# A spectral filter beside an MLP on one core: both outputs of the small-tile transforms in one visit over six PSUM banks

## The chip, the cores and the metric

The kernel runs on one core of a Trainium2 chip. The core has a matrix engine, TensorE (PE in the profile, PEld for its weight loads), which writes only to PSUM, a memory of eight banks of 512 float32 columns by 128 partitions; VectorE (DVE), ScalarE (ACT) and GpSimd (POOL), which work on SBUF (VectorE and ScalarE on PSUM too); and SyncE (SP), which issues most of the transfers. The metric is the device time of one execution in microseconds: 148.74 us before the change, the median of three runs (148.69 to 148.85).

## What is computed

The input has 2048 tokens of 640 columns, in bfloat16. It is normalised, goes through a spectral filter and through an MLP, and the sum of all three is the output:

```python
def _A_ref(x, w_r, w_i):
    X = jnp.fft.rfft2(x.astype(jnp.float32), axes=(-2, -1))
    X = X * (w_r + 1j * w_i)
    return jnp.fft.irfft2(X, s=(S, D), axes=(-2, -1)).astype(jnp.bfloat16)

def _B_ref(x, w1, b1, w2, b2):
    h = _gelu(jnp.einsum("bsd,df->bsf", x, w1) + b1)
    return jnp.einsum("bsf,fd->bsd", h, w2) + b2

xn = _layernorm(x, axis=-1)
return x + _A_ref(xn, A_w_r, A_w_i) + _B_ref(xn, B_w1, B_b1, B_w2, B_b2)
```

The MLP goes from 640 to 1536 columns and back. All Fourier transforms are matmuls with tables of cosines and sines.

## The kernel before

The tokens are split into 16 tiles of 128 (token 16p + c is partition p of tile c). The stages, with the letters that the code and this text use:

- Each tile is normalised (VectorE; GpSimd takes the power) and transposed, tiles 0 to 7 by TensorE (`ps<-ident` in the profile), the others by transfers. The transposed tiles are `xnT`.
- The MLP's first layer runs over five blocks of tiles (4, 2, 2, 4 and 4 tiles) and 12 chunks of columns, five matmuls each (`ps<-xnT,W`); ScalarE applies the gelu and writes `gT`. The second layer takes twelve chunks a tile (`ps<-W,gT`), 512 and 128 columns each. Its result for ten tiles (`KEEP`) is computed early and added to the residual by VectorE ("kept" tiles, `kps`, line 949); for the other six it is computed at the end.
- Stage a folds the normalised tiles along their width and transforms them over the 128 partitions (`ps<-gtab`); the results are `XV`.
- Stage b, the forward width transform (`ps<-etab,XV`), works on a group of two or three tiles of `XV` in a visit of TensorE: per tile four full matmuls of 160 columns, and then, in another tile mode of the array, four remainders on 32 rows each that run side by side. Six visits, b0 to b5. VectorE and ScalarE copy the four banks to `Xb`.
- Stage c is a 16-point transform along the tokens (`ps<-Xb,mtab`): 32 matmuls of 32 x 32 x 322 columns in a visit, in the tile mode that makes 16 small arrays of the one. It has two outputs, r = 0 and 1, and each has its own visit over four banks: c00, c01 to c30, c31. They are copied to `Y`. VectorE multiplies by the filter weights `Wf` and adds (lines 838, 842: `T`, `Z`).
- Stage d is the inverse of c (`ps<-Z,ntab`), 32 matmuls of 320 columns a visit, again two visits for the two outputs v. The copies are `U` (their buffers lie in `gtab`, `T` and `U`), and transfers transpose these back into `XV` (line 863).
- Stage e is the inverse width transform (`ps<-getab`), VectorE unfolds, and the last transform over partitions (`ps<-Wf,htab`) adds into the second layer's banks or, for kept tiles, into banks of its own. VectorE adds the residual and SP writes the tile out.

The program is written as a list of operations with costs, priorities, buffers and dependencies. A planner (`Sched`) runs once when the program is built: it takes at each step the operation that can start first, the one of highest priority among near equals, gives it a buffer or PSUM banks within its `ZONE`, and so fixes the order of each engine and the waits between engines. `LAND` holds the landing times that it assumes for transfers; they enter only the order. `CHAIN` fixes the order of the visits b, c and d. Between two visits the planner puts matmuls of the MLP ("fillers"), while VectorE and ScalarE empty the chain's banks. The chain uses banks 0 to 3; first-layer fillers (`hps`) use banks 4 to 7, and the kept second layer two banks of these at a time.

All matmuls but the transposes are issued by one helper (`mms`, line 518), and the copies by another (`copy`, lines 529 for ScalarE and 530 for VectorE), so a group in the profile is told apart by its tiles: `ps` is PSUM, `W` the weights and later the output tiles.

## Time and profile before

| what | value |
| --- | --- |
| median of three runs | 148.74 us |
| span of the profiled execution | 147.0 us |
| time outside the span | 1.7 us |
| TensorE busy | 141.9 us, 97% |
| VectorE busy | 113.3 us, 77% |
| ScalarE busy | 83.8 us, 57% |
| GpSimd busy | 23.0 us, 16% |
| first, last matmul of the chain b to d | 50 us, 104 us |

The profile is one execution with the hardware profiler on. The span goes from its first to its last instruction; the reported time is 1.7 us longer. A row of the timeline is a start, a duration, and a run of like instructions merged into one; since matmuls overlap in the array, the price of a run is the start of the next row less its own. A few records are missing from a trace; where one is missing the next row has a small gap ahead of it. The busy share of an engine says little by itself: what counts is who waits for whom.

### The profile page before, as it was taken

Reading aid. Unit: us, or ns where it says so; the run is one execution under the profiler, and the core shown is the slowest. Engines: PE = TensorE matmul, PEld = TensorE weight load, DVE = VectorE, ACT = ScalarE, POOL = GpSimd, SP = SyncE. Lnnn points to the kernel's source line nnn. Section 1 sums busy time; section 2 is a strip of 40 time slices with the busy share of each in tenths; the row PEclk is TensorE's granted clock in tenths of the full one; section 3 lists DMA queues with packets and bytes.
Section 4 is the critical chain, followed back from the end, with each engine's and each line's share of the span. In section 5 each row is a group of like instructions: output and inputs, shape, how many; then the busy total and the mean of one; then the engine's idle time right before and its main releaser. Section 6 shows DMA issues by size and latency. Waiting matters only on the chain.

```text
span 147.0 us, 4149 instructions
## 1 busy us (share of the span) xinstructions
PE 141.9 (97%) x1738; PEld 89.8 (61%) x1754; DVE 113.3 (77%) x239; ACT 83.8 (57%) x143; POOL 23.0 (16%) x50
## 2 busy tenths in 40 slices
PE   7999999999999999999999999999999999999993
PEld 7899568898655655656455455334456666566573
DVE  2968999999999254979654796496206999999991
ACT  3123998899989875442878373697766324010300
POOL 4320111420000499400000000000006300000000
DMA  4899999999878899992015205606353951332233
GB/s 128 291 307 409 363 235 224 362 195 170 145 142 159 227 216 252 266 269 71 4 26 116 41 4 115 66 17 122 79 116 73 228 140 45 109 121 89 89 136 92
DMA packets 28995, 23.00 MB, mean 156 GB/s; under 512 B 17840, under 2 KB 25776, under 8 KB 28848
## 3 DMA queue, kind: packets, MB, share of 16 engines
q1 hardware_dynamic: 26640, 17.48, 48.3%
q0 software_dynamic: 2336, 5.25, 15.7%
q8 instruction: 14, 0.23, 0.6%
q14 instruction: 5, 0.04, 0.1%
HBM read 13.54 MB, written 2.62 MB: 110 GB/s over the span
## 4 chain that ended last, share of the span: by engine, by line
PE 93%; DVE 2%; DMA 2%; issue 1%
PE ps L518 92%; PE ps L690 2%; DMA X<-in_A_x_dram 2%; DVE stats L639 1%; DVE U L670 0%; DVE mv L642 0%; DVE W L958 0%
## 5 line engine op out<-in xcount | busy, mean ns | idle before, releaser
L518 PE MATMUL ps<-xnT,W 128*128 128x512 bf16 (+2 forms) x384 | 57.1, 300 | 0.0
L518 PE MATMUL ps<-W,gT 128*128 128x512 bf16 (+3 forms) x382 | 55.5, 292 | 1.4 <-issue 0.9
L518 PEld LDWEIGHTS ps<-W,gT 128*128 128x128 bf16 x396 | 29.9, 98 | 22.9 <-issue 1.9
L518 PEld LDWEIGHTS ps<-xnT,W 128*128 128x128 bf16 x384 | 31.8, 98 | 17.5 <-issue 2.0
L763 ACT ACTIVATE gT<-ps,b1col 128x512 bf16<-128x512 f32 (+1 forms) x60 | 35.0, 616 | 6.1 <-PE ps L518 5.1
L943 POOL DMA_DIRECT2D xnT<-in_A_x_dram x8 | 9.9, 2792 | 51.1 <-DMA XV<-U 51.1
L529 ACT ACTIVATE Wf<-ps 128x960 bf16<-128x960 f32 (+1 forms) x8 | 6.7, 869 | 17.6 <-PE ps L518 17.6
L639 DVE BATCH_NORM_STATS2 stats<-X 128x6 f32<-128x320 bf16 x32 | 13.7, 465 | 2.0 <-DMA X<-in_A_x_dram 2.0
L529 ACT ACTIVATE Xb<-ps 128x960 bf16<-128x960 f32 (+1 forms) x8 | 9.1, 1169 | 6.9 <-PE ps L518 6.7
L838 DVE TENSOR_TENSOR T<-Y,Wf 128x1288 bf16<-128x1288 bf16 x16 | 12.3, 823 | 0.0
L529 ACT ACTIVATE Y<-ps 128x644 bf16<-128x644 f32 x9 | 6.3, 707 | 7.5 <-PE ps L518 7.5
L949 DVE TENSOR_TENSOR X<-ps,X 128x640 f32<-128x640 f32 x8 | 6.5, 819 | 5.0 <-PE ps L518 5.0
L943 POOL DMA_DIRECT2D X<-in_A_x_dram x8 | 7.2, 2080 | 19.4 <-DMA Wf<-in_A_w_i_dram 19.4
L644 POOL TENSOR_TENSOR rstd<-mv,mhalf 128x2 f32<-128x2 f32 (+1 forms) x10 | 6.6, 663 | 20.9 <-DVE mv L642 20.9
L709 DVE TENSOR_TENSOR T<-T 128x512 bf16<-128x512 bf16 (+1 forms) x32 | 8.3, 314 | 0.1
L530 DVE CAST Xb<-ps 128x640 bf16<-128x640 f32 (+1 forms) x4 | 4.3, 1067 | 5.1 <-PE ps L518 5.1
L958 DVE TENSOR_TENSOR W<-ps,xnT 128x640 bf16<-128x640 f32 (+2 forms) x10 | 6.9, 686 | 1.1 <-PE ps L518 1.0
L530 DVE CAST Y<-ps 128x644 bf16<-128x644 f32 x7 | 5.8, 822 | 2.4 <-PE ps L518 2.4
L842 DVE TENSOR_TENSOR Z<-T 128x644 bf16<-128x644 bf16 x16 | 7.0, 486 | 0.8 <-PE ps L518 0.8
L518 PE MATMUL ps<-etab,XV 32*128 32x160 bf16 (+1 forms) x128 | 7.2, 232 | 0.0
L529 ACT ACTIVATE XV<-ps 128x256 bf16<-128x256 f32 (+4 forms) x9 | 6.8, 751 | 0.5 <-PE ps L518 0.5
L897 DVE TENSOR_TENSOR Wf<-Wf 128x960 bf16<-128x960 bf16 (+1 forms) x12 | 6.8, 593 | 0.3 <-ACT Wf L529 0.2
(59 smaller groups left out, 145.6 us busy)
## 6 DMA issues: line engine op xcount, KB each, us to landing
X<-in_A_x_dram POOLq DMA_DIRECT2D x8, 320.0 KB, 6.8
xnT<-in_A_x_dram POOLq DMA_DIRECT2D x8, 320.0 KB, 8.7
out_dram<-W SPq DMA_DIRECT2D x15, 160.0 KB, 1.8
X<-in_A_x_dram SPq DMA_DIRECT2D x6, 320.0 KB, 8.5
W<-in_B_w_dram SPq DMA_DIRECT2D x4, 480.0 KB, 10.4
W<-in_B_w_dram SPq DMA_DIRECT2D x6, 192.0 KB, 3.8
Wf<-in_A_w_r_dram SPq DMA_DIRECT2D x7, 160.5 KB, 10.3
Wf<-in_A_w_i_dram SPq DMA_DIRECT2D x7, 160.5 KB, 9.7
```

Source lines behind the costliest of these rows:

```text
L518: ins = e.matmul(o_, lhsT=lw, rhs=rh, start=st, stop=sp_, skip_group_check=True)
L529: return e.activation(dst(), src(), ACT.Copy, scale=scale)
L530: return e.tensor_copy(dst(), src())
L639: o = K.op([("dve", 0.393)], pr, lambda e, _, c=c, h=h: e.bn_stats(stats[:, c, 6 * h:6 * h + 6], view(X, c * D + H2 * h, [[1, H2]])), read ...
L644: K.op([("pool", 0.65)], 500, lambda e, _, a=a, b=b: e.tensor_tensor(out=rstd[:, a:b], in0=mv[:, a:b, 1], in1=mhalf[:, a:b], op=ALU.pow), ...
L709: ring_ops.append(K.op([("dve", dve_us(4 * w, 2))], pr, lambda e, _, op=op, x1v=x1v, xfv=xfv, o_=o_, o0=o0, o1=o1, w=w: e.tensor_tensor(ou ...
L763: g_op = K.op([("act", act_us(128 * nt, 1))], pr + PRIO["gelu"] + GP[bi], lambda e, _, c0=c0, nt=nt, fc=fc, hps=hps: e.activation(gT[:, fc ...
L838: filt_ops.append(K.op([("dve", dve_us(4 * KP, 2))], pr, lambda e, _, k=k, Y=Y, TB=TB, pair=pair: e.tensor_tensor(out=view(TT, TB.slot * 8 ...
L842: K.op([("dve", dve_us(2 * KP, 2))], pr, lambda e, _, TB=TB, Z=Z, r=r, op=op: e.tensor_tensor(out=view(Zb, Z.slot * 4 * KP + r * KP, [[2 * ...
L897: K.op([("dve", dve_us(320 * n, 2))], pr + 2, lambda e, _, k=k, op=op, yo=yo, y2=y2, n=n: e.tensor_tensor(out=view(Wf, Y2 + y2.slot * 3 * ...
L943: xo_ops[c] = K.op([("pool", 0.9)], 51 - c / 20, lambda e, _, c=c, xov=xov: e.dma_start(xov(0, D), xv[:, c, :], accum_op=ALU.add), reads=[ ...
L958: K.op([("dve", dve_us(w))], 95, lambda e, _, os_=os_, fps=fps, o0=o0, w=w, xov=xov, base=base: e.tensor_tensor(out=view(W1, OST + os_.slo ...
```

## The change

1. *c and d, one visit each per four tiles.* Both outputs are computed in one visit of 96 matmuls over six banks. Four banks hold the first output of 322 (or 320) columns and half of the second one; the other halves, 160 columns each, lie two to a bank in banks 4 and 5. The two halves of the array's rows write to those banks in turn, so the visit is cut into twelve runs of eight matmuls (`M_RUNS`, `N_RUNS`). Its third run ends with an increment of a new semaphore of TensorE, and its ninth run waits for it (`mark`).
2. *b by four tiles.* Four visits of four tiles for six of two or three. The fourth tile's columns lie in banks 4 and 5; the remainders are ordered so that row groups do not meet in a bank, with one more such wait between the first round and the fourth. The fourth tile of `Xb` lies in free places of `T` and `gtab`. Two memsets of their padding join the start, two follow stage a.
3. *Copies.* Each b, c and d visit is emptied by four operations, two for the four banks and two for banks 4 and 5.
4. *Fillers of one bank.* The chain's zone is banks 0 to 5. First-layer fillers of the last two blocks and the kept second layer have banks 6 and 7. A kept tile is computed in two halves of 320 columns, each in one bank, each added by VectorE.
5. *Order.* `CHAIN` has 12 entries for 22. `RANK` gives every operation a new priority, from a search; `LAND` has new values. The order changes everywhere.

```diff
+RANK = """
+428 732 735 708 725 420 419 730 734 329 592 297 284 335 376 299 399 300 279 374 448 364 231 406 222 503 503 503 393 503 503 503 503 503 503 503 503 503 503 503 503 503
...
+""".split()
...
     def schedule(self):
+        for o, r in zip(self.ops, RANK, strict=True):
+            o.prio = int(r)
...
-ZONE = {"hps": [(4, 8)], "bps": [(0, 4)], "cps": [(0, 4)], "dps": [(0, 4)],
-        "eps": [(0, 4)], "fin": [(4, 8), (0, 4)], "fps": [(4, 8)], "tps": [(0, 2), (2, 8)], "aps": ANY, "h0": [(2, 8)], "h1": ANY}
+ZONE = {"hps": [(4, 8)], "hpc": [(6, 8)], "bps": [(0, 6)], "cps": [(0, 6)], "dps": [(0, 6)],
+        "kps": [(6, 8)], "eps": [(0, 4)], "fin": [(4, 8), (0, 4)], "fps": [(4, 8)], "tps": [(0, 2), (2, 8)], "aps": ANY, "h0": [(2, 8)], "h1": ANY}
...
-CHAIN = 'b0 b1 c01 c00 b2 c10 c11 b4 d01 d00 b3 c20 c21 d11 d10 b5 c30 d21 c31 d20 d30 d31'.split()
+CHAIN = 'b0 c0 b1 c1 d0 b2 c2 d1 b3 c3 d2 d3'.split()
...
+M_RUNS = [(0, 0, 0, 0, KP, True), (1, 1, 0, 1, 160, True), (1, 1, 1, 1, 160, False), (0, 0, 1, 0, KP, False), (1, 0, 0, 0, KP, True), (0, 1, 0, 0, 162, False), (1, 0, 1, 0, KP, False),
+          (0, 1, 1, 0, 162, False), (0, 1, 0, 1, 160, False), (1, 1, 0, 0, 162, False), (0, 1, 1, 1, 160, False), (1, 1, 1, 0, 162, False)]
...
         def mms(lst):
             def f(e, _):
-                for o_, lw, rh, st, sp_ in lst():
+                for o_, lw, rh, st, sp_, *mark in lst():
+                    if mark == [1]:
+                        e.wait_ge(K.bank, K.banks)
                     ins = e.matmul(o_, lhsT=lw, rhs=rh, start=st, stop=sp_, skip_group_check=True)
+                    if mark == [0]:
+                        K.banks += 1
+                        ins.then_inc(K.bank, 1)
                 return ins
             return f
...
+        def mark(h, a, b, x, k):
+            return ((1,) if (h, b, k) == (0, 0, 0) else (0,) if (h, b, k) == (1, 1, 7) else ()) if x else ()
...
+        def four(slot, lhs, tab):
+
+            def at(i, g):
+                return psb(slot + g, [[1, Q4]], Q4 * i) if i < 3 else psb(slot + 4 + g // 2, [[1, Q4]], Q4 * (g % 2))
+            main = [(at(i, g), lhs(i, g, 0, 128), tab[:, Q4 * g:Q4 * g + Q4], i == 0 or (i == 3 and g % 2 == 0), False) for g in range(4) for i in range(4)]
+            return main + [(at(i, g), lhs(i, 4, 32 * g, 32), tab[32 * g:32 * g + 32, 4 * Q4:5 * Q4], False, True, *((k // 3,) if (k, g) in ((0, 3), (3, 0)) else ()))
+                           for k in range(4) for g in range(4) for i in [(k - g % 2) % 4]]
...
-            for r in range(2):
-                cps = Buf(f"cps{P}_{r}", psum, 4, ZONE["cps"])
-                zone[f"c{P}{r}"] = pe([("small", 0.335)], PRIO["pc"] - P / 2 + 0.02 * r, lambda P=P, r=r, cps=cps: [
...
+            cps = Buf(f"cps{P}", psum, 6, ZONE["cps"])
+            zone[f"c{P}"] = pe([("small", 0.64)], PRIO["pc"] - P / 2, lambda P=P, cps=cps: [
...
+                for hi, r, v, x, w, st in M_RUNS for pp in range(2) for qq in range(2) for lo in range(2)],
...
+                for x in range(2):
+                    K.op([("act", act_us(320 if x else 968)), ("dve", dve_us(320 if x else 968))], PRIO["pc"] - two[pp] / 5,
...
-                    kps = Buf(f"kps{c}", psum, 2, ZONE["fps"])
...
+                    for o0 in (0, H2):
+                        kps = Buf(f"kps{c}_{o0}", psum, 1, ZONE["kps"])
...
+                        kept_ops.append(K.op([("dve", dve_us(H2))], 30, lambda e, _, kps=kps, xov=xov, o0=o0: e.tensor_tensor(
+                            out=xov(o0, H2), in0=psb(kps.slot, [[1, H2]]), in1=xov(o0, H2), op=ALU.add), reads=[kps, xo1], writes=[xo]))
```

Three places of the new order. The first is TensorE at the start, where tiles 0 to 3 are transposed (`ps<-ident`, tiles 0 and 1 from `U`, 2 and 3 from `T`) among the first layer's matmuls. Before:

```order
L690 MATMUL ps<-ident,U 128x128 x5
L518 MATMUL ps<-xnT,W 128x128 x30
L690 MATMUL ps<-ident,T 128x128 x5
L518 MATMUL ps<-xnT,W 128x128 x6
L518 MATMUL ps<-xnT,W 128x256 x6
L518 MATMUL ps<-xnT,W 128x128 x24
L690 MATMUL ps<-ident,T 128x128 x5
L518 MATMUL ps<-xnT,W 128x128 x12
```

After:

```order
L728 MATMUL ps<-ident,U 128x128 x3
L551 MATMUL ps<-xnT,W 128x128 x30
L551 MATMUL ps<-xnT,W 128x256 x6
L728 MATMUL ps<-ident,T 128x128 x5
L551 MATMUL ps<-xnT,W 128x128 x12
L728 MATMUL ps<-ident,T 128x128 x5
L551 MATMUL ps<-xnT,W 128x128 x44
```

Tile 2's transposes (the first from `T`) moved behind the six matmuls of 256 columns, and the next twelve matmuls already use tile 2.

The second place is TensorE in the chain, around the first visits of d and the b visit behind them. Before (d01, d00, b3):

```order
L518 MATMUL ps<-xnT,W 128x512 x5
L518 MATMUL ps<-Z,ntab 32x320 x32
L518 MATMUL ps<-xnT,W 128x512 x5
L518 MATMUL ps<-Z,ntab 32x320 x32
L518 MATMUL ps<-xnT,W 128x512 x8
L518 MATMUL ps<-etab,XV 128x160 x24
L518 MATMUL ps<-xnT,W 128x512 x2
```

After (d0, b2):

```order
L551 MATMUL ps<-W,gT 128x320 x12
L551 MATMUL ps<-xnT,W 128x512 x5
L551 MATMUL ps<-Z,ntab 32x320 x8
L551 MATMUL ps<-Z,ntab 32x160 x16
L551 MATMUL ps<-Z,ntab 32x320 x16
L551 MATMUL ps<-Z,ntab 32x160 x8
L551 MATMUL ps<-Z,ntab 32x320 x8
L551 MATMUL ps<-Z,ntab 32x160 x40
L551 MATMUL ps<-W,gT 128x320 x21
L551 MATMUL ps<-etab,XV 128x160 x32
L551 MATMUL ps<-W,gT 128x320 x15
```

Two visits of 32 with a filler between them became one of 96, and b takes 32 matmuls for 24.

The third place is VectorE behind the first b visits: it copies b's banks to `Xb` (the fourth tile to `T`), adds a kept tile (`X<-ps,X`), copies c's banks to `Y`, and filters (`T<-Y,Wf`). Before:

```order
L530 CAST Xb<-ps 128x2x2x160
L530 CAST Xb<-ps 128x3x2x160
L949 TENSOR_TENSOR X<-ps,X 128x640 x2
L530 CAST Y<-ps 128x2x322
L838 TENSOR_TENSOR T<-Y,Wf 128x1288 x3
```

After:

```order
L566 CAST Xb<-ps 128x3x2x160
L566 CAST T<-ps 128x2x160
L1011 TENSOR_TENSOR X<-ps,X 128x320
L566 CAST Y<-ps 128x2x160 x2
L895 TENSOR_TENSOR T<-Y,Wf 128x1288 x3
```

One b visit with two copies on VectorE and half a kept tile stand there for two visits with one copy each and two tiles; the large copies to `Y` are ScalarE's.

More of the change, by code (lines that the diff above doesn't have):

```diff
@@ L380, in emit @@
                     o.sem, o.count = sems[e], n
+        self.bank, self.banks = nc.alloc_semaphore("s_bank"), 0
         block = es.enter_context(nc.Block())
@@ L503, in bass_parallel_sum__spectral_gfnet__dense_activation_gelu__prompt_kernel @@
         OST, REM = 0, 4 * D
+        XB3 = 16 * KP + 2 * D
         def psb(slot, dims, off=0, p0=0, n=128):
@@ L793, in bass_parallel_sum__spectral_gfnet__dense_activation_gelu__prompt_kernel, with xbv @@
+        def xbv(xb, i):
+            return (xb3, (xb.slot * 3 + i) * 2 * KP) if i < 3 else (gtab, 2 * D) if xb.slot else (TT, XB3)
+        for k, n in ((KP - 2, 3), (2 * KP - 1, 1)):
+            K.op([("pool", 0.1)], 99, lambda e, _, k=k, n=n: e.memset(view(gtab, 2 * D + k, [[1, n]]), 0.0), writes=[B_xbpad], after=a_ops)
+        for gi in range(4):
+            c0 = 4 * gi
             xb = Buf(f"xb{gi}", p_xb)
-            bps = Buf(f"bps{gi}", psum, 4, ZONE["bps"])
-            pb_ops.append(pe(five_segs(n, 0.07 * n + 0.014), PRIO["pb"] - c0 / 10, lambda c0=c0, n=n, bps=bps: five(
-                bps.slot, n, lambda i, g, p0, k: part(XV, p0, k, 2048 * g + 128 * (c0 + i), [[1, 128]]), etab),
+            bps = Buf(f"bps{gi}", psum, 6, ZONE["bps"])
+            pb_ops.append(pe(five_segs(4, 0.07 * 4 + 0.014), PRIO["pb"] - c0 / 10, lambda c0=c0, bps=bps: four(
+                bps.slot, lambda i, g, p0, k: part(XV, p0, k, 2048 * g + 128 * (c0 + i), [[1, 128]]), etab),
@@ L844, in bass_parallel_sum__spectral_gfnet__dense_activation_gelu__prompt_kernel @@
             B_us = [Buf(f"u{pair}") for pair in two]
[L845 to L854 removed]
+            dps = Buf(f"dps{P}", psum, 6, ZONE["dps"])
```

71 lines of the change are left out of this document (38 added, 33 removed), and 18 rows, old and new, of the table RANK.

## The prediction

> **What bounds the kernel now.** I read the page first: the busy shares, the slices, and the chain that ended last.
>
> ```profile
> span 147.0 us, 4149 instructions
> PE 141.9 (97%) x1738; PEld 89.8 (61%) x1754; DVE 113.3 (77%) x239; ACT 83.8 (57%) x143; POOL 23.0 (16%) x50
> ...
> PE   7999999999999999999999999999999999999993
> ...
> PE 93%; DVE 2%; DMA 2%; issue 1%
> PE ps L518 92%; PE ps L690 2%; DMA X<-in_A_x_dram 2%; DVE stats L639 1%; DVE U L670 0%; DVE mv L642 0%; DVE W L958 0%
> ```
>
> TensorE is busy in every slice from the second to the last but one, and 92% of the chain lies on line 518, which issues nearly all its matmuls. The next view is the waits of TensorE alone.
>
> ```profile
> PE ps L518 <- issue: 1.1, 7, 0.2
> ```
>
> Beside it the view has only a wait at the very start: after that TensorE waits for no engine. (The 1.1 us of "issue" stand where a record of a matmul is missing.) So the time is a start, one dense stream of matmuls, and a short tail. The sum is made against the profiled execution: span 147.0 us, 1.7 us below the 148.74 us median; I take that 1.7 us and the tail after the last matmul as unchanged. A shorter stream shortens the time one for one; a faster VectorE or ScalarE gives nothing; a new wait of TensorE adds one for one. TensorE's timeline in two stretches of the spectral chain gives the prices; the first column is the start, so a price is one start less the one before.
>
> ```profile
> 68.35 1.31 PE L518 MATMUL ps<-etab,XV 128*128 128x160 bf16 x24
> 69.59 1.80 PE L518 MATMUL ps<-W,gT 128*128 128x512 bf16 x12
> 71.23 1.24 PE L518 MATMUL ps<-xnT,W 128*128 128x512 bf16 x5
> 72.41 0.51 PE L518 MATMUL ps<-Z,ntab 32*32 32x320 bf16 x32
> 72.85 1.25 PE L518 MATMUL ps<-xnT,W 128*128 128x512 bf16 x5
> 74.06 0.52 PE L518 MATMUL ps<-Z,ntab 32*32 32x320 bf16 x32
> 74.51 1.90 PE L518 MATMUL ps<-xnT,W 128*128 128x512 bf16 x8
> 76.25 1.31 PE L518 MATMUL ps<-etab,XV 128*128 128x160 bf16 x24
> ...
> 88.26 0.98 PE L518 MATMUL ps<-etab,XV 128*128 128x160 bf16 x16
> 89.17 1.80 PE L518 MATMUL ps<-W,gT 128*128 128x512 bf16 x12
> 90.90 0.49 PE L518 MATMUL ps<-Xb,mtab 32*32 32x322 bf16 x32
> 91.33 1.90 PE L518 MATMUL ps<-xnT,W 128*128 128x512 bf16 x8
> ```
>
> A 512-column matmul costs 0.217 us (8 of them from 74.51 to 76.25), so 0.42 ns a column. Six pairs of 512 and 128 columns cost 1.64 us between full matmuls (69.59 to 71.23) and 1.73 us ahead of a small-tile visit (89.17 to 90.90): entering costs 0.09 to 0.10 us. A c visit then takes 0.43 us (90.90 to 91.33) and a d visit 0.44 to 0.45 us (72.41 to 72.85), and 0.01 us more falls on the first full matmul behind it. Of this, columns are two rounds of 322 at 0.42 ns, 0.27 us. What a visit costs beyond its columns is therefore 0.09 + 0.43 + 0.01 - 0.27 = 0.26 us for c, and 0.28 us for d.
>
> **The change, part by part.** *One c and one d visit where there were two.* The columns stay, the fixed part is paid once: 4 x 0.26 + 4 x 0.28 = 2.16 us saved. *Four width visits for six.* These rows give the price of 160 and of 320 columns.
>
> ```profile
> 140.65 0.98 PE L518 MATMUL ps<-W,gT 128*128 128x320 bf16 x6
> 141.46 0.43 PE L518 MATMUL ps<-Wf,htab 128*128 128x512 bf16 x2
> ...
> 142.68 0.99 PE L518 MATMUL ps<-W,gT 128*128 128x160 bf16 x12
> 143.51 0.23 PE L518 MATMUL ps<-Wf,htab 128*128 128x160 bf16 x1
> ```
>
> A 160-column matmul costs 0.069 us (12 in 0.83). A tile of a width visit is four of them and one more time slot for its four 32-row remainders, which run side by side: 0.346 us. The three-tile visit at 68.35 took 1.24 us and the two-tile one at 88.26 took 0.91 us, so the fixed part is 0.20 and 0.22 us, with the 0.01 us behind it 0.22 us. Two fewer visits save 0.44 us. *One-bank fillers.* Two 320-column matmuls cost 2 x 0.135 us (six in 0.81), the 512 and 128 pair 0.273 us (1.64/6): nothing, for all ten tiles. Saved in all: 2.60 us.
>
> *The wait inside a visit.* TensorE now waits for its own semaphore once in each b, c and d visit, because two row groups share a bank there; the matmul that waits, and all that is queued behind it on TensorE, stands until an earlier matmul of the same visit has ended. No wait of this kind is in the trace; the nearest rows are its two halves.
>
> ```profile
> L518 PE MATMUL ps<-Xb,mtab 32*32 32x322 bf16 x256 | 4.0, 301 | 0.0
> L518 PE MATMUL ps<-etab,XV 32*128 32x160 bf16 x64 | 2.2, 231 | 0.0
> ...
> 52.31 1.31 PE L518 MATMUL ps<-etab,XV 128*128 128x160 bf16 x24
> 53.67 1.25 DVE L530 CAST Xb<-ps 128x960 bf16<-128x960 f32 x1 [1.51 <-PE ps L518]
> ...
> 57.45 0.49 PE L518 MATMUL ps<-Xb,mtab 32*32 32x322 bf16 x32
> 58.05 0.71 ACT L529 ACTIVATE Y<-ps 128x644 bf16<-128x644 f32 x1 [0.85 <-PE ps L518]
> ...
> 5.33 0.28 DVE U L670
> 5.61 0.05 issue
> 5.65 0.39 PE ps L690 x2
> ```
>
> A reader starts 0.11 us after the last small-tile record ends (57.94 to 58.05) and 0.05 us after the last 32-row one (53.62 to 53.67); TensorE starts 0.04 us after a release (5.61 to 5.65). In a c or d visit the signal comes from the last matmul of the third run of eight, which starts some 0.12 us in (16 issues of about 3 ns and one pass of 160 columns); its record of 160 columns lasts 0.301 less 0.07, 0.23 us; less the reader's own start, of which I take 0.02 us, the ninth run can start at 0.12 + 0.23 + 0.13 = 0.48 us. Its own turn, behind two rounds of 322 and two of 162 columns (0.41 us) and some 0.03 us of issue, is at 0.44 us. That is 0.04 us for each of eight visits, 0.32 us. In a width visit the signal leaves with the first round of remainders and is needed by the fourth: 0.01 + 0.231 + 0.07 = 0.31 us against a turn at 3 x 0.07 = 0.21 us, so 0.10 us, four times, 0.40 us. Ends for both kinds together: nothing, if the signal leaves before the modelled end of a record, and 0.2 us each, 2.4 us in all, if TensorE's queue fills anew behind the wait. I take the small values: the start 0.04 us behind a release is the same engine and the same step.
>
> [...]
>
> *The start.* In the new order tile 2's transposes stand directly ahead of their first use, where six matmuls of 128 columns and six of 256 stood between.
>
> ```profile
> 9.12 0.44 PE L690 MATMUL ps<-ident,T 128*128 128x128 bf16 x5
> 9.40 2.49 PE L518 MATMUL ps<-xnT,W 128*128 128x128 bf16 x36
> 11.73 0.44 PE L690 MATMUL ps<-ident,T 128*128 128x128 bf16 x5
> ...
> 12.05 0.29 DVE L530 COPY xnT<-ps 128x256 bf16<-128x256 bf16 x1 [0.34 <-PE ps L690]
> ```
>
> Unhindered, the first use comes 12.05 + 0.29 + 0.04 - 11.73 = 0.65 us after the first transpose, of which the five transposes fill 0.28 us (9.12 to 9.40). The stall is 0.37 us; the old order lost some 0.05 us at tile 3 (six matmuls between), which goes. I put down 0.30 us, with 0 and 0.4 us as ends.
>
> *The evacuations.* Six banks are filled at once and have to be emptied before the next visit may write them; what is late next after the switches are the copies out of PSUM.
>
> ```profile
> 51.28 0.89 ACT L529 ACTIVATE Xb<-ps 128x640 bf16<-128x640 f32 x1
> 53.67 1.27 ACT L529 ACTIVATE Xb<-ps 128x960 bf16<-128x960 f32 x1 [0.53 <-PE ps L518]
> ...
> 104.86 2.52 SPq L863 DMA_TRANSPOSE XV<-T  x2
> ...
> 111.40 1.74 ACT L529 ACTIVATE W<-XV 128x384 bf16<-128x384 bf16 x2 [2.19 <-DMA XV<-U]
> ```
>
> After b0 each of two engines copies three tiles and one: 1.27 us and, by the step from 640 to 960 columns, about 0.51 us: 1.78 us. With 0.05 us to start and 0.04 us to release, c0 may start 1.87 us after b0's last record ends. TensorE's filler there is five 512s and six 320s, 5 x 0.217 + 6 x 0.135 = 1.9 us. It just fits. Behind the last d visit the transposes of four outputs, 1.3 us of issue each, and their landing take 111.40 - 104.86 = 6.5 us; with the evacuation of the larger part of an output ahead of them (768 and 192 columns, some 1.1 us by the 0.71 us for 644) and 0.1 us to start, 7.7 us. The filler between d3 and e0 is 51 matmuls of 320, five of 512 and three pairs, 6.9 + 1.1 + 0.8 = 8.8 us: also covered. If a cover is gone, the price is the difference. For the few places with less than 0.2 us to spare I put down 0.10 us in all, with 0 and 1.0 us as ends.
>
> *The rest.* Ten adds of 640 columns become twenty of 320 on VectorE, 1 to 2 us more work. VectorE sat idle 5.0 us ahead of the old ones, waiting for TensorE, which hides it:
>
> ```profile
> L949 DVE TENSOR_TENSOR X<-ps,X 128x640 f32<-128x640 f32 x8 | 6.5, 819 | 5.0 <-PE ps L518 5.0
> ```
>
> On VectorE's queue these adds stand ahead of copies out of Y's banks, and they wait for transfers of POOL's queue; counted at the prices above, b0 comes 0.8 us later in the stream than before, so these transfers have no less time. SP's weight loads and token transposes trade places far ahead of their users. Four memsets more on POOL, 16% busy, cost nothing.
>
> Sum: -2.60 + 0.32 + 0.40 + 0.30 + 0.10 = -1.48 us, 147.26 us; I say 147.3 us.
>
> **The rivals.** *The waits cost nothing* and all is covered: -2.60 + 0.30, 146.4 us. For it: the records' ends are modelled. Against: a reader has never started before such an end.
> *Each matmul has a price of its own* in the issue: eight visits of 96 for sixteen of 32 are 256 more, and the 0.16 us that a c visit of 0.43 us takes beyond its columns bounds the price at 5 ns: 1.3 us on top, 148.5 us. For it: nothing shows how much of the 0.16 us is issue. Against: width visits with 8 or 12 small matmuls have a fixed part nearly as large, 0.22 us. [...]
> *The wait drains the array*, so that each c and d visit pays its fixed part twice: the 2.16 us are lost, and the 0.32 us with them are contained in that, -0.44 + 0.40 + 0.30 + 0.10 = +0.36 us, 149.1 us, slower. It decides from about 0.23 us a visit on (0.04 + 1.48/8). For it: nothing in the trace shows a wait of TensorE on itself in mid visit. Against: after a release it starts in 0.04 us, and the tile mode does not change.
> *The two filler banks run short.* Fillers had four banks and now have two, and the gelu that empties one stands in ScalarE's queue behind the wider Y copies. There are eleven gaps in the chain; from 1.48/11 = 0.13 us a gap the gain is gone, at 0.3 us the time is 147.3 + 3.3 = 150.6 us. For it: ScalarE is in these copies for 0.7 to 1.3 us at a time. Against: TensorE never waited for a bank before, and a bank takes 1.1 us or more to fill.
>
> **How the numbers follow.** Less than 0.2%, 0.3 us, is about what a measurement of this kernel cannot tell from no change. My forecast (146.7 to 148.0 us) has 57%; hidden waits 13%; a price per matmul 7%; the drain, slower, 9%; short banks 10%, of which 4% end within 0.2% and 6% slower; something else late, a transfer above all, 4%, slower. Faster 0.77, same 0.04, slower 0.19. From 146.2 to 149.3 us only the short banks at their worst, half of the 4% and a tail below are left out, some 13%.
>
> **What would show it.** Right: TensorE's timeline has c and d visits of 0.70 to 0.78 us from start to next start, width visits of 1.6 to 1.75 us, a gap of 0.35 us near 10.5 us after tile 2's transposes, and no other wait; the span is near 145.5 us. Wrong: visits of 0.9 us or more (drain), waits of TensorE for ScalarE's gelu or copies between visits (banks), or a gap ahead of e0 that a transfer ends.

## The result, and the profile after

The change makes the kernel slower: 155.71 us median of four runs (155.24 to 156.63) against 148.73 us, a ratio of 1.047 [1.044, 1.051]. The forecast was 147.3 us, with a range that ended at 149.3 us. The profiled execution has a span of 153.9 us, 6.9 us above that of before. Its page:

```profile
span 153.9 us, 4697 instructions
PE 146.6 (95%) x2004; PEld 100.2 (65%) x2010; DVE 116.5 (76%) x257; ACT 80.2 (52%) x139; POOL 23.1 (15%) x54
...
PE   7999999983999999999999999999999999999993
...
PEclk9999999998699999999999999999999999999999
...
PE 77%; DVE 15%; DMA 4%; issue 1%; POOL 1%
```

TensorE was busy in every slice but the ends before; now it has a hole in the ninth and tenth slices (8 and 3 in the row of PE), and the granted clock (the row PEclk) is low in the tenth and eleventh (8 and 6). The chain that ended last is no longer TensorE alone: up to the hole it runs through VectorE and a transfer. The waits of TensorE name that transfer:

```profile
PE ps L551 <- DMA xnT<-U: 2.7, 1, 2.7
...
PE ps L551 <- issue: 0.3, 2, 0.2
```

It is the transpose of tile 15, from SP's queue, which the first layer of the last block of tiles needs. TensorE's timeline there:

```profile
33.51 0.71 PE L551 MATMUL ps<-xnT,W 128*128 128x256 bf16 x5
36.96 7.90 PE L551 MATMUL ps<-xnT,W 128*128 128x512 bf16 x33 [2.74 <-DMA xnT<-U]
...
49.76 1.00 PE L551 MATMUL ps<-gtab,T 128*128 128x128 bf16 x15
```

and the windows of 2 us over it (the columns: length, busy time and count of PE, PEld, DVE, ACT, POOL, then the granted clock of TensorE, the DMA share and GB/s):

```profile
34.00:36.00 2.00, 0.22 (x3) 0.00 (x0) 1.54 (x6) 1.25 (x2) 0.00 (x0) 1.00 1.23 113
36.00:38.00 2.00, 1.04 (x6) 0.62 (x7) 1.97 (x8) 0.00 (x0) 0.39 (x1) 0.92 0.71 157
38.00:40.00 2.00, 2.00 (x6) 0.70 (x5) 1.97 (x7) 1.80 (x4) 0.42 (x1) 0.50 0.93 157
40.00:42.00 2.00, 2.00 (x10) 0.95 (x9) 0.66 (x2) 1.18 (x3) 0.00 (x0) 0.72 1.30 199
```

The wait is 2.7 us, and behind it the mean granted clock is 0.50 from 38 to 40 us and 0.72 from 40 to 42 us: 2 x 0.50 + 2 x 0.28 = 1.6 us of lost work. So 4.3 of the 6.9 us are lost here, long before the part of the program that the change is about.

The visits themselves, in the same timeline (start, duration; b0 and the filler behind it, c0 from its first matmul to the filler behind it, then a filler and d0):

```profile
56.03 1.78 PE L551 MATMUL ps<-etab,XV 128*128 128x160 bf16 x32
57.74 1.25 PE L551 MATMUL ps<-xnT,W 128*128 128x512 bf16 x5
...
59.74 0.32 PE L551 MATMUL ps<-Xb,mtab 32*32 32x322 bf16 x6
...
60.84 2.33 PE L551 MATMUL ps<-xnT,W 128*128 128x512 bf16 x10
...
71.77 1.24 PE L551 MATMUL ps<-xnT,W 128*128 128x512 bf16 x5
72.95 1.20 PE L551 MATMUL ps<-Z,ntab 32*32 32x320 bf16 x96
```

The c visit takes 60.84 - 59.74 = 1.10 us from start to next start; the prediction said 0.70 to 0.78, and "wrong" from 0.9 on. The d visits take 1.13 to 1.16 us, and one c visit took 1.52 us. With 0.10 us to enter and 0.01 us behind, and less the columns (0.54 us), the eight visits cost 6.05 us beyond their columns; the sixteen of before cost 4.4 us. That is 1.6 us more, where 1.84 us less (2.16 saved, 0.32 for the wait) were expected. Of the 1.6 us some 0.4 is one gap in the visit of 1.52 us, whose cause is another (below); 1.2 us are left to the visits themselves. The b visit takes 57.74 - 56.03 = 1.71 us, inside the predicted 1.6 to 1.75.

So the 6.9 us are: 4.3 for the late transpose and the clock behind it, 1.6 for the c and d visits, 0.4 to 0.5 for the start, and some 0.5 that is spread.

### The profile page after: what moved, and what is told of

It is laid out like the page before. It is cut to its first block, busy times and chain, and to the rows that moved or that the text cites. A ratio compares the mean times of both kernels' runs of the same rounds, so it can differ in the third digit from the quotient of the medians.

```text
span 153.9 us, 4697 instructions
## 1 busy us (share of the span) xinstructions
PE 146.6 (95%) x2004; PEld 100.2 (65%) x2010; DVE 116.5 (76%) x257; ACT 80.2 (52%) x139; POOL 23.1 (15%) x54
## 4 chain that ended last, share of the span: by engine, by line
PE 77%; DVE 15%; DMA 4%; issue 1%; POOL 1%
PE ps L551 76%; DVE stats L677 6%; DMA xnT<-U 3%; DVE T L743 2%; DVE T L747 2%; DMA X<-in_A_x_dram 2%; DVE U L708 1%; DVE mv L680 1%; DVE xnT L566 1%; POOL rstd L682 1%; PE ps L728 1%; DVE XV L566 1%; DVE T L708 0%; DVE W L1020 0%
## 5 line engine op out<-in xcount | busy, mean ns | idle before, releaser
L551 PE MATMUL ps<-W,gT 128*128 128x320 bf16 (+3 forms) x390 | 56.8, 294 | 0.5 <-issue 0.3
L551 PEld LDWEIGHTS ps<-W,gT 128*128 128x128 bf16 x396 | 34.6, 98 | 18.2 <-ACT gT L801 0.2
L747 DVE TENSOR_TENSOR T<-T 128x128 bf16<-128x128 bf16 (+1 forms) x32 | 8.7, 316 | 5.0 <-PE ps L551 4.8
L1011 DVE TENSOR_TENSOR X<-ps,X 128x320 f32<-128x320 f32 x16 | 7.8, 487 | 5.6 <-PE ps L551 5.4
L565 ACT ACTIVATE Y<-ps 128x968 bf16<-128x968 f32 (+1 forms) x8 | 6.4, 839 | 3.8 <-PE ps L551 3.8
L566 DVE CAST Y<-ps 128x320 bf16<-128x320 f32 (+1 forms) x8 | 4.9, 655 | 4.6 <-PE ps L551 4.6
L566 DVE CAST Wf<-ps 128x960 bf16<-128x960 f32 (+1 forms) x5 | 5.4, 1085 | 2.7 <-PE ps L551 2.6
L566 DVE CAST Xb<-ps 128x960 bf16<-128x960 f32 x4 | 4.9, 1232 | 3.2 <-PE ps L551 3.2
L551 PE MATMUL ps<-etab,XV 128*128 128x160 bf16 (+1 forms) x128 | 7.1, 233 | 0.0
L551 PE MATMUL ps<-Wf,htab 128*128 128x512 bf16 (+3 forms) x33 | 7.0, 296 | 0.0
```

Source lines behind the costliest of these rows:

```text
L551: ins = e.matmul(o_, lhsT=lw, rhs=rh, start=st, stop=sp_, skip_group_check=True)
L565: return e.activation(dst(), src(), ACT.Copy, scale=scale)
L566: return e.tensor_copy(dst(), src())
L747: ring_ops.append(K.op([("dve", dve_us(4 * w, 2))], pr, lambda e, _, op=op, x1v=x1v, xfv=xfv, o_=o_, o0=o0, o1=o1, w=w: e.tensor_tensor(ou ...
L1011: kept_ops.append(K.op([("dve", dve_us(H2))], 30, lambda e, _, kps=kps, xov=xov, o0=o0: e.tensor_tensor(out=xov(o0, H2), in0=psb(kps.slot, ...
```

## The experiments

Two theories followed. One: TensorE cannot issue 96 small matmuls as fast as their columns would allow. Two: the new order asks for the transposes too early. The rivals: the self-wait or the shared banks make the visits slow; the stall in front is only a symptom.

**What a small matmul costs.** The first kernel leaves the old order, banks and visits as they are, has no wait inside, and only cuts each c and d matmul in two.

```diff
-(psb(cps.slot + 2 * pp + hi, [[1, KP]], 0, 64 * qq + 32 * (lo ^ pp), 32),
+(psb(cps.slot + 2 * pp + hi, [[1, 161]], 161 * y, 64 * qq + 32 * (lo ^ pp), 32),
...
-for v in range(2) for pp, qq, hi, lo in tiles],
+for v in range(2) for y in range(2) for pp, qq, hi, lo in tiles],
```

> The kernel before, with every c and d matmul cut into two of half the columns (161 or 160): 64 matmuls a visit for 32, the same columns, banks and outputs, and no wait inside. Theory A, TensorE issues small matmuls quickly (some 3.3 ns apart) only up to about 32, and then one every 8.5 ns: the last of 64 starts 32 x 8.5 ns = 0.27 us later than the 32nd, of which some 0.1 us lie beside columns, so a visit takes 0.6 us for 0.43, and 16 of them add 2.4 us or more: 151 us (150.5 to 153). Rival B, issue is not what makes the new visits slow (their shared banks or the wait are): 32 more matmuls of 3.3 ns at most, hidden beside the columns, and the time stays within 0.5 us of 148.7.

Measured: 154.96 us median (153.53 to 155.15), a ratio of 1.038 [1.032, 1.045]. This is slower than either theory said. Its timeline at a c visit:

```profile
55.28 0.76 PE L518 MATMUL ps<-Xb,mtab 32*32 32x161 bf16 x64
55.98 1.80 PE L518 MATMUL ps<-W,gT 128*128 128x512 bf16 x12
```

A visit takes 55.98 - 55.28 = 0.70 us for 0.43, so 0.27 us more for 32 more matmuls and the same columns; sixteen of them make 4.3 us. (The remaining 2 us are two gaps, which make one c visit 1.08 us and one b visit 0.34 us longer, and a wait of 0.8 us for VectorE; the gaps are explained below.) The second kernel keeps the 64 matmuls and makes the 33rd wait for the 32nd:

```diff
-for o_, lw, rh, st, sp_ in lst():
+for k, (o_, lw, rh, st, sp_) in enumerate(lst()):
+    half = len(lst()) == 64
+    if half and k == 32:
+        e.wait_ge(K.bank, K.banks)
     ins = e.matmul(o_, lhsT=lw, rhs=rh, start=st, stop=sp_, skip_group_check=True)
+    if half and k == 31:
+        K.banks += 1
+        ins.then_inc(K.bank, 1)
```

> The kernel with the halved c and d matmuls (64 a visit), with one wait more in each visit: the 33rd matmul waits for a signal of the 32nd. Theory A, TensorE's sequencer hands on some 32 pairs of weight load and matmul that were queued while the matmuls ahead ran, and feeds the rest at 8.35 ns apiece: while the 33rd waits, the queue fills behind it, so the last 32 start 3 to 4 ns apart and not 8.35 (0.10 to 0.15 us from the 33rd to the 64th, for 0.258); the wait itself costs a pass and the signal's way, so the 33rd starts some 0.45 to 0.5 us into the visit for 0.267, and a visit takes 0.75 to 0.85 us for 0.694. Rival B, it is the array or the bank, not the feed, that makes the later matmuls slow: they stay 8.35 ns apart behind the wait too, and a visit takes 0.9 us.

```profile
55.09 0.36 PE L522 MATMUL ps<-Xb,mtab 32*32 32x161 bf16 x32
55.64 0.36 PE L522 MATMUL ps<-Xb,mtab 32*32 32x161 bf16 x32 [0.20 <-PE ps L522]
55.94 1.80 PE L522 MATMUL ps<-W,gT 128*128 128x512 bf16 x12
```

The two halves have the same length, 0.36 us; a visit takes 0.85 us, and the one run 157.13 us. The third kernel is the changed one with its c and d matmuls cut to 16 columns:

```diff
-(psb(cps.slot + (4 + pp if x else 2 * pp + hi), [[1, w]], (160 * hi if x else r * KP), 64 * qq + 32 * (lo ^ pp), 32),
+(psb(cps.slot + (4 + pp if x else 2 * pp + hi), [[1, 16]], (160 * hi if x else r * KP), 64 * qq + 32 * (lo ^ pp), 32),
```

> The changed kernel, with every matmul of the c and d visits cut to its first 16 columns: the 96 matmuls, their banks and the wait inside stay, most of the columns of stages c and d are not computed. Theory A, the issue sets the length of a visit: 32 x 3.3 ns and 64 x 8.5 ns make 0.65 us, with some 0.1 us to enter and 0.1 us to end about 0.8 us, so a visit falls only from 1.1 to 0.75 to 0.95 us. Rival B, the columns or the meeting of row groups in a bank set it: a visit falls to 0.45 us or less, eight of them by 5 us in all.

```profile
70.65 0.93 PE L551 MATMUL ps<-Z,ntab 32*32 32x16 bf16 x96
71.51 1.26 PE L551 MATMUL ps<-W,gT 128*128 128x320 bf16 x8
```

A visit with a twentieth to a tenth of the columns still takes 0.86 us, as theory A said (the one run: 153.09 us). From the records of the traces, the median over all visits of a kernel, when the k-th matmul of a visit starts (us from its first):

```
kernel                        16th   17th   32nd   33rd   last   next full matmul
before, 32 a visit            0.050  0.149  0.202    -      -    0.444
halved, 64                    0.050  0.082  0.134  0.267  0.526  0.695
halved, with the wait, 64     0.050  0.081  0.135  0.556  0.692  0.854
16 columns, 96                0.050  0.065  0.122  0.205  0.755  0.864
changed kernel, 96            0.050  0.109  0.175  0.334  0.961  1.130
```

The first 16 start 3.3 ns apart in every kernel (0.050/15). Behind the 32nd there is a pause of 0.08 to 0.16 us, and from the 33rd on they start 8.3 ns apart in the halved kernel ((0.526 - 0.267)/31) and 8.7 ns with 16 columns, so columns do not set it. With the wait ahead of the 33rd, those behind it start 4.4 ns apart again ((0.692 - 0.556)/31), their 0.136 us equal to the 0.134 us of the first 32, as theory A said of this kernel. So the array can take them quickly. A reading that fits, an estimate from these numbers, is that some 32 pairs of weight load and matmul are ready ahead and a further pair comes each 8.3 ns: the pace changes behind the 32nd pair in all three kernels that have more and no wait there. No trace shows such a store itself, and what sets the pause behind the 32nd was not tried. The old visits have 32, and so never showed what more of them would cost. In the changed kernel 64 of 96 matmuls lie beyond: at the 8.3 ns of the halved kernel 64 x 8.3 = 0.53 us of the visit's 1.13, and 0.334 + 63 x 0.0083 = 0.86 us stand as a floor for the start of the last one; the pass itself takes 0.17 us more. The remaining 0.1 us are short steps at the ninth run, where the self-wait stands, and at changes of width.

**What the late transposes come from.** The planner had taken the transposes of tiles 12 to 15 to land about 3 us after their issue; they took 7.39, 5.61, 5.53 and 3.95 us. The next kernel only tells it so.

```diff
-"xnT12#0": 3.04, "xnT13#0": 2.93, "xnT14#0": 3.55, "xnT15#0": 2.94
+"xnT12#0": 7.39, "xnT13#0": 5.61, "xnT14#0": 5.53, "xnT15#0": 3.95
```

> The changed kernel, with one thing other: the planner is told that the transposed tiles 12 to 15 land 7.39, 5.61, 5.53 and 3.95 us after their transfers are issued (what the profile of the changed kernel shows) instead of 3.04, 2.93, 3.55 and 2.94. Theory A, the order took these transfers for faster than they are: the 2.74 us in which TensorE waits for a transposed tile near 34 us goes, and with it the 1.5 us or so that the lowered clock (0.74 between 38 and 44 us) cost: 155.7 - 4.3 = 151.4 us (150.6 to 152.4), and the granted clock stays at 0.97 or more in every 2 us stretch between 30 and 45 us. Rival B, the stall is only a symptom and TensorE would run into the next late thing: 155.7 us, less 1 us at most. The c and d visits stay as they are (1.1 us) by both.

Measured: 155.41 us (154.88 to 158.47), a ratio of 1.043 [1.036, 1.049]: theory A fell in this form. The order came out much the same, and the transposes went out 1.1 us later than before, so that the wait stayed. (Its profile is of the execution of 158.47 us, with a mean granted clock of 0.989; the four others had 1.00, and their waits are not on record.) SP's queue of the changed kernel, then of this one, and its wait:

```profile
19.30 4.14 SPq L544 DMA_DIRECT2D W<-in_B_w_dram  x4
26.41 4.44 SPq L717 DMA_TRANSPOSE xnT<-T  x2
30.90 3.30 SPq L717 DMA_TRANSPOSE xnT<-U  x2
```

```profile
27.55 4.67 SPq L717 DMA_TRANSPOSE xnT<-T  x2
32.27 3.30 SPq L717 DMA_TRANSPOSE xnT<-U  x2
```

```profile
PE ps L551 <- DMA xnT<-U: 2.5, 1, 2.5
```

In both, four transposes take 7.8 us and more of SP's time, though the last of them takes 1.28 us in the changed kernel. What stands ahead of them are the weights of the second layer, 1.9 MB. In the kernel before, the first two transposes behind these weights took even longer, but TensorE waited for none:

```profile
24.77 5.53 SPq L679 DMA_TRANSPOSE xnT<-T  x2
```

The next kernel issues the weights behind the transposes:

```diff
+        for o in w2_ops:
+            o.gate.append(TD[15])
         K.schedule()
```

> The changed kernel, with one thing moved: the four loads of the second layer's weights (480 KB each), which stand on SP's queue directly ahead of the transposes of tiles 12 to 15, are issued behind the transpose of tile 15; nothing needs these weights before 51 us. All else has the same order up to the chain. Theory A, the transposes are late because they are issued and move behind 1.9 MB of weights (2.0 to 2.3 us of issue each for the first three, where an undisturbed one takes 1.28): issued from 26.4 us at 1.28 us apiece tile 15's goes out at 30.3 us, 2.6 us sooner than the 32.9 us of the changed kernel, and lands near 34 us, where TensorE first needs it: the wait of 2.74 us shrinks to 0.5 us or less, the clock stays at 1.00, and the time is 155.7 - 4.2 = 151.5 us (150.8 to 152.2). Rival B, the transposes take their time whatever stands ahead of them, or the weights now come too late: the wait of 2 us or more stays or moves to the second layer, 154.5 us or more. By both the time stays above 148.7 us, since the c and d visits stay at 1.1 us.

```profile
26.27 2.62 SPq L719 DMA_TRANSPOSE xnT<-T  x2
28.94 2.60 SPq L719 DMA_TRANSPOSE xnT<-U  x2
31.59 2.17 SPq L544 DMA_DIRECT2D W<-in_B_w_dram  x4
```

```profile
33.41 6.76 PE L551 MATMUL ps<-xnT,W 128*128 128x256 bf16 x38
...
45.10 1.00 PE L551 MATMUL ps<-gtab,T 128*128 128x128 bf16 x15
...
69.05 0.71 PE L551 MATMUL ps<-Z,ntab 32*32 32x320 bf16 x45
71.81 0.92 PE L551 MATMUL ps<-Z,ntab 32*32 32x160 bf16 x51 [2.05 <-issue]
72.66 4.26 PE L551 MATMUL ps<-W,gT 128*128 128x320 bf16 x21
```

The mechanism was right: the transposes take 1.3 us each, TensorE does not wait, and the fifteen matmuls that began at 49.76 us begin at 45.10, 4.7 us sooner. The time is 155.87 us (155.52 to 156.20) all the same, ratio 1.048 [1.044, 1.051]; the number of theory A was missed by 4.4 us. The gain is lost again by 81 us, where the third c visit begins at 80.60 us for 80.79: TensorE stands 2.05 us in the middle of the first d visit, waiting for nothing that the profile shows, then the mean granted clock is 0.72 from 70 to 74 us and 0.85 from 74 to 78 us, and ahead of that TensorE waits 0.7 us near 57 us.

**What TensorE waited for in mid visit.** Such a gap, "issue" in the view of waits, is in most kernels of this study: 0.43 us in the changed one (a c visit of 1.52 us), 0.41 and 1.17 us in the halved, 0.80 us in the one with 16 columns, each from the start of one matmul or weight load to the next. By the counts, TensorE's instructions come by a queue of their own (q8, "instruction", 16 KB at a time; it has 14 such transfers before, 16 in the changed and 18 in the halved kernel, whose pages count 3492, 4014 and 4532 matmuls and weight loads, one transfer for each 256 begun). Counted from the first (a weight load, a matmul and a wait for a semaphore in TensorE's records are one each), the gaps lie as follows; "in hand" is the time from the begin of the transfer of the next 16 KB to the last instruction before the gap, "asked late" the time from the entry into the block before to the begin of that transfer:

```
kernel                  instructions done   gap    in hand   asked late
changed                 1473                0.43   1.81      5.72
halved                  1473                0.41   1.82      3.58
halved                  1729                1.17   1.13      4.95
16 columns              2241                0.80   1.79      1.41
weights late            1729                2.31   0.14      4.94
changed, next block     1729                0      4.02      1.04
before, its shortest    1473                0      5.51      2.41
```

1473, 1729 and 2241 differ by whole multiples of 256. TensorE goes on 2.2 to 2.6 us after the transfer began in all five (gap and time in hand together). The reading that fits is that it ran out of instructions: the table has them in blocks of 256, the transfer of the next block beginning while the current one runs. In the kernel before no gap lies at such a boundary in the chain (5.51 us in hand at the least); two things differ here. The visits of 96 use a block in as little as 3.6 us (80.81 to 84.40 us in the changed kernel, 3.2 us in the one with 16 columns), where before it lasted 6.5 us and more in the chain. And a transfer that begins 1.0 to 1.6 us after the block before it is entered at five other boundaries of the changed kernel (transfers between 54.33 and 85.67 us) began up to 5.7 us after. What stood in the DMA queues then, in the kernel with the late weights from the entry into the block (64.4 us) to the transfer (69.35 us), and from there to the end of the gap:

```profile
q0 software_dynamic: 576, 1.31, 112.7%
...
X<-in_A_x_dram POOLq DMA_DIRECT2D x1, 320.0 KB, 7.4
```

```profile
q0 software_dynamic: 221, 0.49, 80.0%
q8 instruction: 1, 0.02, 2.2%
```

Beside the one transfer of instructions only GpSimd's transfers of the residual, whose packets took 112.7% and then 80.0% of the 16 engines' time. Two kernels on top of the late weights spread these out: the first makes them wait for the additions of the kept tiles, the second lets no more than two be under way.

```diff
+        for i, t in enumerate(KEEP[3:]):
+            xo_ops[t].deps.append(kept_ops[2 * i + 1])
```

> The kernel with the late weights, and GpSimd's transfers of the residual spread out: from the fourth kept tile on, each waits for the addition of the kept tile three before it, so that they no longer stand in the DMA queues all at once between 56 and 71 us. TensorE's instructions have the same order. Theory A, TensorE ran out of instructions: its gaps in mid visit (2.31 us at 69.49 us with the late weights, 0.43 us at 67.89 us in the changed kernel) lie where its 1729th or 1473rd instruction ends, a whole number of 256 apart, and the transfer of the next 16 KB of instructions had begun only 0.14 and 1.81 us before, 4.9 and 5.7 us after the block before was entered, behind GpSimd's transfers; elsewhere it begins some 1 us after. With those spread out no such transfer begins more than 2.5 us after its block is entered, no gap over 0.2 us lies at such a boundary, the granted clock is 1.00 in every 4 us stretch from 50 us on, and the time falls by the 2.3 us and the 1.5 us that the lowered clock cost behind it: 155.9 - 3.8 = 152.1 us (151.0 to 152.8). Rival B, the gap has another cause (the wait of TensorE on itself, a filter step of VectorE): it stays in the visit of d0, 155 us or more.

```diff
+        seq = list(KEEP) + [t for t in range(16) if t not in KEEP]
+        for a, b in zip(seq, seq[2:]):
+            xo_ops[b].deps.append(xo_ops[a])
```

> The same with another spreading: each of GpSimd's residual transfers waits for the landing of the one two before it, so that at most two are in flight. Theory A: the same, no gap at a block's end and 152.1 us (151.0 to 153.0); a transfer that is needed by a kept tile may come late, which would show as a wait of TensorE for VectorE's addition. Rival B: 155 us or more, with the gap in mid visit.

With the first, no transfer of instructions in the chain begins more than 2.3 us after its block is entered, the visit of d0 takes 1.13 us, and the longest gap at a block's end is 0.30 us (2.30 us in hand). But a new wait took the place of the old one, for the addition of the first kept tile, whose transfer GpSimd held back (TensorE's wait, and GpSimd's queue):

```profile
PE ps L551 <- DVE X L1013: 2.9, 1, 2.9
```

```profile
54.62 2.72 POOL L1006 DMA_DIRECT2D X<-in_A_x_dram  x3 [6.03 <-DMA Wf<-in_A_w_i_dram]
```

Its executions scatter from 152.99 us, with a mean granted clock of 1.00, to 157.75 us, with 0.976, so that no ratio can be given; the mechanism of theory A held but for the 0.30 us, its number did not. The second gave 154.34 us (152.69 to 157.35); its three executions with a mean granted clock of 1.00 took 152.69 to 154.34 us, ratio 1.030 [1.025, 1.034]. In its profile, which is of the execution of 157.35 us, the gap moved from block 1729 to block 2241 and was longer, 3.6 us, with a transfer that began 4.8 us after the entry, 1.3 us into the gap. There residual transfers and SP's transposes were under way together, and four of the latter took 14 us of issue:

```profile
75.23 14.03 SPq L926 DMA_TRANSPOSE XV<-U  x4
```

So two under way seem still too many beside transposes. The next two kernels keep the first spreading and let the first three kept tiles' transfers go sooner: from 37 us on in the first, behind the transposes of tiles 8 to 11 and the issue of the last filter weights in the second.

```diff
-            xo_ops[c].gate += [WL[-1], TD[15]]
-            xo_ops[c].deps += WL + list(TD.values())
+            xo_ops[c].gate += [TD[15]] if c in KEEP[:3] else [WL[-1], TD[15]]
+            xo_ops[c].deps += [] if c in KEEP[:3] else WL + list(TD.values())
```

> The kernel with the late weights and the spread residual transfers, and the residual transfers of the first three kept tiles no longer wait for the landing of the last filter weights: they go out from about 37 us on. In the run with the spread transfers TensorE stood 2.9 us near 57 us until VectorE had added the first kept tile, whose transfer had been held back by 6.0 us for these weights. Theory A, all that is left of the change then is the visits and the start: no wait of TensorE over 0.5 us behind 12 us, no gap at a block's end, clock 1.00 throughout. The eight c and d visits cost 8 x 0.69 = 5.5 us beyond their columns where the sixteen of the kernel before cost 4.4 us: +1.1; the start +0.4; small waits at the fillers +0.3 to +0.5: 148.7 + 1.9 = 150.6 us (150.0 to 151.5), slower than before with nothing late at all. Rival B, another transfer or another engine is late next and the time stays at 152.5 us or more. Rival C, the visits do win once nothing is late: 148.7 us or less.

```profile
PE ps L551 <- DMA xnT<-T: 6.3, 1, 6.3
```

```profile
36.70 12.57 SPq L719 DMA_TRANSPOSE xnT<-T  x4
```

It became the slowest of these, 159.63 us (158.56 to 162.28), ratio 1.068 [1.064, 1.072]: rival B. Again four transposes beside residual transfers take more than 12 us of issue. The second:

```diff
-            xo_ops[c].gate += [TD[15]] if c in KEEP[:3] else [WL[-1], TD[15]]
-            xo_ops[c].deps += [] if c in KEEP[:3] else WL + list(TD.values())
+            xo_ops[c].gate += [WL[-1], TD[15]]
+            xo_ops[c].deps += list(TD.values()) if c in KEEP[:3] else WL + list(TD.values())
```

> As the kernel with the early residual transfers, but those of the first three kept tiles now wait until the last filter weights are issued (not landed) and until the transposes of tiles 8 to 15 have landed: they go out from about 48 us on, behind the transposes that stood for 12.6 us of issue beside the early ones, and some 5 us ahead of the 53.8 us of the late weights kernel. Theory A, nothing is late any more: no wait of TensorE over 0.5 us behind 12 us, no gap at a block's end, clock 1.00; what is left is 8 x 0.69 - 4.4 = +1.1 us for the c and d visits, +0.4 for the start, +0.3 to +0.5 for small waits: 150.6 us (150.0 to 151.5). Rival B, a transfer is late next in this order too: 152.5 us or more. Rival C, the visits win once nothing is late: 148.7 us or less.

```profile
span 149.7 us, 4711 instructions
...
PEclk9999999999999999999999999999999999999999
```

```profile
PE ps L551 <- DVE X L1013: 0.4, 1, 0.4
PE ps L551 <- DVE xnT L566: 0.2, 1, 0.2
```

151.58 us (151.09 to 152.21), ratio 1.019 [1.015, 1.022], 4.1 us faster than the changed kernel and 2.8 us slower than before; it is 1.0 us above the number of theory A and just past its range. No wait over 0.5 us is left behind 12 us, and one gap of 0.33 us at a block's end, as in the first spreading. Of the 2.7 us by which its span exceeds that of before, the c and d visits are 1.4 (5.81 us beyond their columns for 4.4; 0.2 of it is that gap, so 1.2 are again the visits themselves), the start 0.6, the wait for the addition with what it drags along 0.56. With no wait over 0.5 us left the change is still a loss.

**The change without the searched order.** One kernel has the visits, copies and fillers, but neither the table of priorities nor the new landing times.

```diff
-        for o, r in zip(self.ops, RANK, strict=True):
-            o.prio = int(r)
```

> The changed kernel without the fifth part: no table of priorities, and the landing times of the kernel before; the visits over six banks, b by four tiles, the copies and the one-bank fillers stay. Theory A, the late transfers come from the searched order, and the visits are slow by themselves: no wait of 2 us for a transposed tile, clock near 1 in every stretch, c and d visits of 1.1 us as in the changed kernel; the time is 148.7 + 1.6 (the visits, against those of the kernel before) and what an order that was not fitted loses, 150 to 152.5 us. Rival B, the order is not to blame: 155 us or more, with the same wait.

```profile
PE ps L549 <- DVE T L745: 4.6, 3, 1.9
PE ps L549 <- ACT Xb L563: 2.9, 1, 2.9
```

173.04 us (172.00 to 174.79), ratio 1.159 [1.151, 1.167]; both theories missed. No wait for a transposed tile is in it, and the d visits take 1.12 to 1.13 us, as expected; but b0 and c0, b1 and c1 follow each other with no filler between, and TensorE waits for the copies. So the transposes' lateness came with the fifth part, the searched order and its landing times, and this experiment says nothing on how good an order the change could have had.

## Why the prediction was wrong

- *One c and one d visit where there were two*: the step that failed for the visits, 2.16 us saved as forecast, with the wait 1.84, and 1.6 us lost as measured (1.4 in the last of the kernels with moved transfers; 1.2 in both without the gaps at a block's end). The fixed part is indeed paid once: entering costs 0.10 us as before. The step took 0.16 us a visit of 32 as a bound on what issuing costs. It is no bound for 96: the 32nd starts 0.12 to 0.20 us behind the first, and those beyond start 8.3 ns and more apart.
- The rival "each matmul has a price of its own", at 7%, was the right mechanism. Its size was not: 5 ns at most for each of 256 more, where 512 of the 768 matmuls in the new visits lie beyond the 32nd and start 10.0 ns apart in the mean ((0.961 - 0.334)/63; 8.3 ns in the halved kernel). By the prediction's own 0.3 us its 148.5 us would have been no change, though its chance stands among the faster.
- *The rest*: "SP's weight loads and token transposes trade places far ahead of their users" was put at nothing. This is the other step that failed, at 4.3 us. The 2.7 us of wait and the 1.6 us of the lowered clock behind it take its place. The profile of before had a sign of it: two transposes behind 1.9 MB of weights on the same queue took 5.53 us. "Something late, a transfer above all" had 4%, with no place named.
- *The waits inside a visit*: right for b, 0.35 us beyond its columns for 0.23, so 0.12 us where 0.10 was said; four visits for six saved nothing and cost nothing, -0.44 + 0.48. In c and d the 0.04 us can't be told from the issue. Doubly paid fixed parts, the drain, did not happen: the wait alone, put into the halved kernel, starts its matmul 0.42 us after the one it waits for and makes the visit 0.16 us longer (0.854 for 0.695), less than a second fixed part of 0.26 to 0.28 us.
- *The start*: TensorE's first use of tile 2 comes 10.92 - 10.25 = 0.67 us after its first transpose (0.65 said), 0.39 us of stall at the predicted place:

```profile
10.25 0.44 PE L728 MATMUL ps<-ident,T 128*128 128x128 bf16 x5
10.92 0.84 PE L551 MATMUL ps<-xnT,W 128*128 128x128 bf16 x12 [0.22 <-DVE xnT L566]
```

- *One-bank fillers* and *the evacuations*: as forecast. No wait of TensorE in the changed kernel is for a bank, ahead of e0 or for the gelu, so the rival of the short banks fell, at least with 6.9 us more time for the copies. Where the transposes came in time, TensorE did wait for additions that empty a filler's bank: 0.7 us with the late weights, since the residual's transfer landed late, and 0.4 us in the last of these kernels, since the addition stood on VectorE behind a copy that waited for a transfer. "These transfers have no less time" held only while the other wait came first.
- The supply of instructions was in none of the cases. It cost 0.43 us in the changed kernel, and up to 3.6 us in kernels where it fell on another transfer.

## What to carry to other kernels

In these kernels a burst of small matmuls was cheap up to about 32 pairs of weight load and matmul (the 32nd started 0.12 to 0.20 us behind the first), and cost 8.3 to 10.0 ns each beyond, as much as 20 to 24 columns at 0.42 ns: cutting outputs to fit banks, so that fewer visits hold more and narrower matmuls, paid the saved switch back and more. Where an order is moved, go through the transfers that the moved work waits for, with all that stands ahead of them on their queue and beside them on the engines. The denser stream of instructions used up its blocks of 256 sooner (one in 3.6 us, where it had been 6.5 us and more); TensorE went on 2.2 to 2.6 us after the begin of the next one's transfer, and with the late weights that transfer came 4.9 us after the entry, while GpSimd's took 112.7% of the 16 engines' time.

## What was not expected of the hardware

- The first 16 small matmuls of a visit started 3.3 ns apart and the 32nd 0.12 to 0.20 us behind the first; from the 33rd on they started 8.3 ns (halved), 8.7 ns (16 columns) and 10.0 ns apart (changed kernel), with a pause of 0.08 to 0.16 us ahead of it.
- TensorE ran out of instructions in a straight program, as the counts read: gaps of 0.3 to 3.6 us at counts that differ by whole multiples of 256 instructions; in the five of the table it went on 2.2 to 2.6 us after the begin of a 16 KB transfer of instructions.
- Behind an idle time of 2.7 us the mean granted clock was 0.50 for 2 us and 0.72 for 2 more; with one of 2.05 us, of the late weights, it was 0.72 and 0.85 in the windows of 4 us from 70 us on; with one of 2.3 us in the kernel with 16 columns, at the same place as the first, it was 1.00 in every window of 2 us from 32 to 46 us. So the length of the idle time alone does not decide it; what else does was not tried.
- Transposes beside accumulating transfers of GpSimd took 3.1 to 3.5 us of issue each, for 1.28 us, the median of `xnT<-T` in the changed kernel (12.57 and 14.03 us for four). Seen twice; by what it comes was not tried.
